# Talking-heads attention and two MLPs on one core: cosine's argument in turns, and all weights of the second MLP made float32 beside the first

## The chip, the core and the metric

The kernel runs on one core of a Trainium2 chip. The core has a matrix engine (TensorE: PE for its matmuls, PEld for the weight loads that run beside them), a vector engine (DVE), a scalar engine (ACT), GpSimd (POOL) and a queue of transfers that SyncE (SP) issues. Each engine takes its instructions strictly in the order in which they stand in its queue. An instruction that waits therefore holds everything behind it on that engine. The metric is the device time of one execution in microseconds (us), as the median of several runs.

## What is computed

All inputs are float32 or float64 arrays; the weights of both MLPs arrive as float64 and are used as float32. With 4 sequences of 448 tokens, 12 heads of 64:

```python
# attention with mixed heads
scores = q @ k.T / 8;  scores = einsum('bhij,hg->bgij', scores, w_pre)
attn = softmax(scores);  attn = einsum('bhij,hg->bgij', attn, w_post)
x = attn @ v                        # 1792 tokens x 768
# first MLP: 768 -> 2048 -> 768
h = x @ w_in;  g = h * cos(h);  y = g @ w_out
# second MLP: 768 -> 768 -> 768
h = maximum(maximum(y @ w1, y @ w2), y @ w3);  return h @ w_out
```

The names `moe_w_in`, `moe_w_out` belong to the first MLP, `moe2_w1` to `moe2_w3` and `moe2_w_out` (in the kernel `w_out2`) to the second.

## The kernel before

Activations are kept transposed: features on the 128 partitions, 448 tokens of one sequence in the free dimension. Every product is made from three matmuls with operands cut in a high and a low part (`three`, L191 to L195): high by high, low by high, high by low. So every tensor that enters a product is first cut: ACT casts the high part, and DVE or POOL subtracts it to get the low part.

Three stages follow each other. Attention has an order worked out by a planner from costs and due times (`Plan`, and the `add` calls in `attention`); it takes the span to about 500 us and is hardly touched here. The planner also places the first MLP's start, and its table of the steps of the cosine is the last part of the diff.

The first MLP (`layers`) runs over 8 groups of two hidden blocks, and in each over the 4 sequences: 32 steps. One step makes two hidden blocks of 128 features (36 matmuls), sends each through `times_cos`, and multiplies the result of the step before with w_out (36 matmuls), whose six results DVE adds to `acc`. A hidden block stays in PSUM until the cosine's product (`times`, L233) has read it. PSUM has 8 banks and a step takes 8 of them in turn, so the first hidden block of a step takes the bank that the first hidden block of the step before has left.

`times_cos` makes h*cos(h) in nine instructions. ACT writes h/2pi plus a large constant, which rounds it to whole turns (L216), and takes the constant off again (L219). DVE subtracts that many turns from h in two instructions, once with a short constant C1 and once with the rest C2 (both L224). ACT takes the size (L227) and the sine of pi/2 minus it (L230). DVE multiplies by h (L233), ACT casts the high part (L236), DVE makes the low one (L239).

Weights come as float64. One half row block (128 x 384 numbers) is loaded raw (384 KB), and an ACT and four DVE instructions make it float32. This happens at two places: in `weight_steps` (L130 to L146), just ahead of the weight's use, and in `float32_block` (L316 to L322), which makes a block and stores it in DRAM (L323) to be loaded later as float32 (192 KB, L312). Both use the same two buffers for raw data. In this text such a half block with its four DVE instructions is one conversion.

The second MLP takes two sequences at a time (p = 0, 1). It uses Strassen's scheme with 7 products for each of w1 to w3: `tokens` makes the token side (sums of quarters, each cut in high and low), `unit_weights` the weight side (L335 sums, L340 and L341 cuts), `unit` the 7 products p1 to p7. `unit` is run for 3 pairs of output blocks (j) and 3 weights (wi), so 9 times per p; the largest of the three is cut and multiplied with w_out2 in `out_product`, which is run for two sequences per j. `tokens` has 33 subtractions per p: 12 sums and 21 low parts, of which every third is on POOL (L365).

Of the 36 blocks of w1 to w3, `rest` converts 22 beside the first MLP (BEFORE, L472) and 14 in the first half of the second, two per unit (L486). The 12 half blocks of w_out2 are converted where they are used (L521), once for each p: 24 conversions. `tokens(0)` stands behind the first MLP's loop, `tokens(1)` behind the units of p = 0 (L480); the products with w_out2 of the last j of p = 0 come in the course of p = 1.

The order of the MLPs' instructions on each engine is made by a scheduler from the program's order and costs of its own, so a row of the code doesn't tell the place in a queue. The places that matter are shown as rows of the queues with the change.

Of the kernel before, what the change touches and what calls it, by code (L numbers as in the profile page):

```python
# [9 lines left out]
F32 = mybir.dt.float32  # L10
# [8 lines left out]
DM = H * D  # L19
# [14 lines left out]
KH = KC // 2  # L34
BEFORE = 22
FC = DFF // 128
NB = NT // S
TWO_PI = 2.0 * math.pi
C1 = 6.28125
C2 = TWO_PI - C1  # L40
ROUND = 1.5 * 2.0 ** 23
# [3 lines left out]
def f32(ap):  # L45
    return ap.bitcast(F32)


@with_exitstack
def talking_heads_mlps(ctx, tc, q, k, v, w_pre, w_post, same_row, w_in, w_out, w1, w2, w3, w_out2, outT):  # L50
    nc = tc.nc
    dram = ctx.enter_context(tc.tile_pool(name="dram", bufs=1, space=bass.MemoryType.DRAM))
    xT = dram.tile([DM, NT], F32, name="xT")

    tp = ctx.enter_context(tc.tile_pool(name="t", bufs=2, side="right", reuse_waits="tile"))
    mlps = Mlps(ctx, tc, xT, tp, w_in, w_out, (w1, w2, w3), w_out2, outT)
    mlps.kept = {(i, f): dram.tile([128, DM], F32, name=f"w{i}_{f}") for i in range(3) for f in range(KC)}
    with tc.manual_schedule(), ExitStack() as att:
        behind = attention(att, tc, q, k, v, w_pre, w_post, same_row, xT, tp, mlps)
    for ins in behind:  # L60
        ctx.enter_context(tc.issue_after(ins))
    mlps.rest()
# [7 lines left out]
class Mlps:  # L70
# [138 lines left out]
    def times_cos(self, pos, g, f):  # L209
# [10 lines left out]

        def less(c):
            if c == C1:
                o["r"] = self.tile("r", [128, S], F32)
            nc.vector.scalar_tensor_tensor(o["r"], o["k"], -c, h if c == C1 else o["r"], op0=ALU.mult, op1=ALU.add)  # L224

# [3 lines left out]
        def cos():  # L229
            nc.scalar.activation(o["r"], o["r"], AF.Sin, bias=self.half_pi, scale=-1.0)  # L230

# [8 lines left out]

        return [turns, whole, lambda: less(C1), lambda: less(C2), size, cos, times, high, low]

# [58 lines left out]
    def float32_block(self, src, keep=False):  # L301
# [3 lines left out]
        n = KH * 128  # L305
        w, kept = (x[:, c * n:(c + 1) * n] for x in (self.w123[wi][f], self.kept[wi, f]))
        float64 = w.dtype != F32
# [42 lines left out]
    def tokens(self, p):  # L350
# [3 lines left out]
        if p == 0:  # L354
            xs = [h for _ in range(3) for h in self.two_parts()]
            self.B = {x: halves(t) for x, t in zip(("11", "T1", "T2", "21", "T3", "T4"), xs)}
            self.outs = (lambda t: [t[:, :KC], t[:, KC:]])(self.tile("x", [128, 2 * KC, S], F32))
        y = {(r + 1, n + 1): self.acc[2 * p + n][:, r * KH:(r + 1) * KH] for r in range(2) for n in range(2)}
        turn = [0]

        def parts(x, c, src):
            hi, lo = (t[:, c] for t in self.B[x])
            nc.scalar.copy(hi, src)
            turn[0] += 1
            (nc.vector if turn[0] % 3 else nc.gpsimd).tensor_sub(lo, src, f32(hi))  # L365

# [93 lines left out]
    def rest(self):  # L460
        self.late = self.pools("late", "left")
        self.acc = [None] * NB
        self.spare = None
        blocks = [(wi, 2 * j + f, c) for j in range(KC // 2) for wi in range(3) for f in range(2) for c in range(2)]
        before = A = None
        first = self.layers(self.x, [(self.w_in[f],) for f in range(FC)], self.w_out, self.times_cos, self.to_y, self.GROUPS)
        steps = FC // self.GROUPS * NB
        for i, product in enumerate(first):
            if before:
                before()  # L470
            before = product
            while i > 1 and 36 - len(blocks) < BEFORE * (i - 1) / (steps - 4):  # L472
                self.float32_block(blocks.pop(0), True)
            if i == steps - 3:
                A = self.unit_weights(0, 0)
        ends, outs = [], [before]
        for p in range(NB // 2):
            run(ends)
            ends = []
            self.tokens(p)  # L480
            for j in range(KC // 2):
                most = {x: self.tile("kr"[i % 2], [128, S], F32) for i, x in enumerate(("11", "12", "21", "22"))}
                for wi in range(3):
                    p1, p5, p6, p2, p7, p4, p3 = self.unit(A or self.unit_weights(j, wi), wi, most)
                    A = None
                    for src in blocks[:2]:  # L486
                        self.float32_block(blocks.pop(0), True)
                    run([p1, p5])
# [29 lines left out]
                def outs_of(n, p=p, j=j, g=g, wo=wo, accs=self.outs):  # L518
                    if not wo:
                        self.spare = None  # L520
                        wo += [self.weight(self.w_out2[f]) for f in (2 * j, 2 * j + 1)]  # L521
                    self.out_product(2 * p + n, j, g[n], wo, accs[n])
# [76 lines left out]
def attention(ctx, tc, q, k, v, w_pre, w_post, same_row, xT, tp, mlps):  # L599
# [293 lines left out]
    for n in range(2):  # L893
# [3 lines left out]
        for c in range(KC):  # L897
            add(xhi, (n, c), r + 2.0 + c * RANK["fxgap"], {"A": 0.467}, [("xget", n)])
            add(xlo, (n, c), r + 2.0 + c * RANK["fxgap"], {"P": 1.09, "V": 0.535}, [("xhi", n, c)])
    acts = ({"A": 0.424}, {"A": 0.467}, {"V": 0.535}, {"V": 0.535}, {"A": 0.467}, {"A": 0.56}, {"V": 0.535}, {"A": 0.467}, {"V": 0.535})  # L900
    for f in range(FG):
        for c in range(KC):
            add(hidden, (f, c), r0 + RANK["fh"] + (f * KC + c) * RANK["fhgap"], {"T": 0.567},
                [("wcut", f, c // (KC // 2), 6), ("xlo", 0, c)] + ([("hidden", f, c - 1)] if c else [])
                + ([("act", f - 1, 6)] if f and c == 0 and BUFS["ps_x"] == 1 else []))
        for y, e in enumerate(acts):
            add(act, (f, y), r0 + RANK["fa"] + f + y * 0.2, e, [("act", f, y - 1) if y else ("hidden", f, KC - 1)]
                + [("soft", i) for i in range(N)] * (y == 5) + [("act", f - 1, 0)] * (f and y == 0))

# [47 lines left out]
```

## Time and profile before

| | us |
|---|---|
| median of 3 runs (lowest, highest) | 1353.25 (1352.34, 1357.11) |
| the profiled execution | 1349.79 |
| its span, first to last instruction | 1348.0 |
| PE busy / PEld busy | 1278.1 (95%) / 1056.2 (78%) |
| DVE / ACT / POOL busy | 1111.8 (82%) / 765.0 (57%) / 322.9 (24%) |

Matmuls are pipelined, so that a matmul shown with 0.37 us starts about 0.2 us after the one before it. Busy time of PE is therefore not its distance from full use; the count of matmuls in a stretch is. A wait in a row is the idle time of the engine before the instruction, and the arrow names the instruction whose end released it. The granted clock is a share of full speed: 1.00 is 2.4 GHz, 0.50 is 1.2 GHz.

### The profile page before, as it was taken

The numbers are of one execution on the slowest core, as the hardware profiler recorded it, in microseconds if no ns is written. First come the engines' busy times: TensorE is split into PE (matmuls) and PEld (weight loads), VectorE is DVE, ScalarE is ACT, GpSimd is POOL, SyncE is SP. The second block draws the span as 40 slices with busy tenths as digits, with TensorE's granted clock in tenths as the row PEclk, the third lists the DMA queues.
The fourth block names the chain that finished last, engine by engine and source line by source line (L and its number), as shares of the span: only waits on it lengthen the run. The fifth ranks groups of instructions, "written<-read, shape, count | busy, mean of one in ns | idle before, by whom it ended". The sixth has DMA issues, their size and how long they took to land. (4 is left out here: it accounts for less than half of the span.)

```text
span 1348.0 us, 20632 instructions
## 1 busy us (share of the span) xinstructions
PE 1278.1 (95%) x7002; PEld 1056.2 (78%) x7002; DVE 1111.8 (82%) x2276; ACT 765.0 (57%) x1697; POOL 322.9 (24%) x273
## 2 busy tenths in 40 slices
PE   7999999999999889999999999999979999899998
PEld 2676666676677668889888889999968888688988
DVE  1888787887878897899999989977889959988585
ACT  3877776776777777754554545535544444524440
POOL 0000010000100135221111111212255645645450
PEclk8999999999999999999999999999989999899999
DMA  6753444344343444533333333213024422134122
GB/s 206 198 160 95 123 137 141 112 121 127 108 123 101 127 122 151 141 88 112 104 90 95 94 88 88 71 48 95 8 84 144 118 71 60 47 118 129 47 77 82
DMA packets 81310, 143.09 MB, mean 106 GB/s; under 512 B 8789, under 2 KB 62645, under 8 KB 81205
## 3 DMA queue, kind: packets, MB, share of 16 engines
q1 hardware_dynamic: 81205, 141.78, 35.5%
q8 instruction: 55, 0.90, 0.3%
q14 instruction: 50, 0.41, 0.1%
HBM read 84.95 MB, written 18.09 MB: 76 GB/s over the span
## 5 line engine op out<-in xcount | busy, mean ns | idle before, releaser
L193 PE MATMUL ps<-x,w 128*128 128x448 f32 x708 | 266.3, 377 | 35.9 <-DVE r L233 12.0
L195 PE MATMUL ps<-x,w 128*128 128x448 f32 x708 | 262.4, 372 | 2.7 <-DVE x L176 0.8
L194 PE MATMUL ps<-x,w 128*128 128x448 f32 x708 | 262.4, 371 | 0.6 <-POOL w L152 0.6
L733 PEld LDWEIGHTS aps<-w2s,e 120*112 120x112 f32 x1440 | 164.1, 177 | 52.6 <-issue 20.2
L193 PE MATMUL ps<-gh,w 128*128 128x448 f32 x528 | 193.8, 367 | 1.5 <-DVE x L456 1.5
L194 PE MATMUL ps<-gh,w 128*128 128x448 f32 x528 | 193.4, 366 | 0.0
L195 PE MATMUL ps<-gl,w 128*128 128x448 f32 x528 | 193.2, 366 | 0.1
L733 PE MATMUL aps<-w2s,e 120*112 120x120 f32 x1440 | 179.8, 271 | 9.9 <-DVE w2s L728 6.9
L152 POOL TENSOR_TENSOR w<-wf,w 128x384 fp32r<-128x384 f32 x88 | 101.7, 1169 | 364.9 <-ACT w L149 309.0
L341 POOL TENSOR_TENSOR w<-wf,w 128x384 fp32r<-128x384 f32 x126 | 149.3, 1204 | 147.8 <-ACT w L340 112.8
L193 PEld LDWEIGHTS ps<-x,w 128*128 128x128 f32 x708 | 135.2, 191 | 59.4 <-DVE r L233 16.8
L195 PEld LDWEIGHTS ps<-x,w 128*128 128x128 f32 x708 | 135.3, 191 | 17.4 <-DVE x L365 2.3
L194 PEld LDWEIGHTS ps<-x,w 128*128 128x128 f32 x708 | 135.7, 192 | 11.8 <-POOL w L152 0.9
L711 DVE TENSOR_REDUCE nm<-mps 120x1 f32<-120x448 f32 x180 | 111.5, 620 | 36.6 <-PE mps L707 33.0
L716 ACT ACTIVATE e<-mps,nm 120x448 f32<-120x448 f32 x180 | 114.4, 636 | 41.1 <-DVE nm L711 32.4
L700 POOL TENSOR_TENSOR tl<-t,th 120x448 fp32r<-120x448 f32 x22 | 26.4, 1200 | 437.9 <-ACT th L615 292.7
L193 PEld LDWEIGHTS ps<-gh,w 128*128 128x128 f32 x528 | 99.2, 188 | 10.4 <-DVE x L456 1.9
L195 PEld LDWEIGHTS ps<-gl,w 128*128 128x128 f32 x528 | 99.2, 188 | 9.0 <-DVE gl L239 0.4
L194 PEld LDWEIGHTS ps<-gh,w 128*128 128x128 f32 x528 | 99.2, 188 | 8.1
L615 ACT CAST th<-t 120x448 fp32r<-120x448 f32 x167 | 94.3, 567 | 19.6 <-DMA t<-s 6.0
L340 ACT CAST w<-wf 128x384 fp32r<-128x384 f32 x126 | 61.0, 513 | 77.3 <-DVE wf L335 27.2
L700 DVE TENSOR_TENSOR tl<-t,th 120x448 fp32r<-120x448 f32 x158 | 100.3, 635 | 2.3 <-ACT th L615 2.0
(107 smaller groups left out, 2348.7 us busy)
## 6 DMA issues: line engine op xcount, KB each, us to landing
t<-s SPq DMA_DIRECT2D x144, 192.5 KB
wraw<-in_w_out_dram SPq DMA_DIRECT2D x56, 384.0 KB
wraw<-in_w_dram SPq DMA_DIRECT2D x36, 384.0 KB
wf<-w SPq DMA_DIRECT2D x72, 192.0 KB
wraw<-in_w_in_dram SPq DMA_DIRECT2D x32, 384.0 KB
t<-s SPq DMA_DIRECT2D x48, 210.0 KB
w<-wf SPq DMA_DIRECT2D x36, 192.0 KB
q<-in_q_dram SPq DMA_DIRECT2D x48, 112.0 KB
```

The costliest lines, as they stand in the source:

```text
L152: nc.gpsimd.tensor_sub(lo, chunks(o["f"]), f32(hi))
L193: mm(w[0], x[0], start=first, stop=False)
L194: mm(w[1], x[0], start=False, stop=False)
L195: mm(w[0], x[1], start=False, stop=last)
L340: nc.scalar.copy(hi, w)
L341: nc.gpsimd.tensor_sub(lo, w, f32(hi))
L615: copy = lambda eng, *a: nc.scalar.copy(*a) if eng == "A" else any_of[eng].tensor_copy(*a)
L700: any_of[eng].tensor_sub(live["tl", i], live["t", n][:P, t, :], f32(live["th", i]))
L711: nc.vector.tensor_reduce(nm, live["m", i][:P], axis=AX.X, op=ALU.max, negate=True)
L716: nc.scalar.activation(e, live["m", i][:P], AF.Exp, bias=live["nm", i], scale=1.0, accum_out=z)
L733: nc.tensor.matmul(ps[:JC, j], live["e", i][:, j * JC:(j + 1) * JC], live["w2s", i], start=True, stop=True)
```

## The change

The cosine's argument is taken in turns: one DVE instruction makes h/2pi minus the whole turns, and the sine gets the factor 2pi as its scale. `times_cos` has eight steps instead of nine. All 48 blocks of the second MLP's weights, those of w_out2 among them, are made float32 beside the first MLP, from step 4 on, 48 of them over 28 steps; the second MLP only loads float32. `unit_weights(0, 0)` moves one step ahead, `tokens(0)` moves from behind the loop to the step before the last, all 21 low parts of `tokens` are on DVE, and at p = 1 the remaining products with w_out2 come ahead of `tokens(1)`.

```diff
@@ times_cos
-        def less(c):
-            if c == C1:
-                o["r"] = self.tile("r", [128, S], F32)
-            nc.vector.scalar_tensor_tensor(o["r"], o["k"], -c, h if c == C1 else o["r"], op0=ALU.mult, op1=ALU.add)
+        def part_of_turn():
+            o["r"] = self.tile("r", [128, S], F32)
+            nc.vector.scalar_tensor_tensor(o["r"], h, 1.0 / TWO_PI, o["k"], op0=ALU.mult, op1=ALU.subtract)
...
-            nc.scalar.activation(o["r"], o["r"], AF.Sin, bias=self.half_pi, scale=-1.0)
+            nc.scalar.activation(o["r"], o["r"], AF.Sin, bias=self.half_pi, scale=-TWO_PI)
...
-        return [turns, whole, lambda: less(C1), lambda: less(C2), size, cos, times, high, low]
+        return [turns, whole, part_of_turn, size, cos, times, high, low]
@@ float32_block
-        w, kept = (x[:, c * n:(c + 1) * n] for x in (self.w123[wi][f], self.kept[wi, f]))
+        w, kept = (x[:, c * n:(c + 1) * n] for x in ((*self.w123, self.w_out2)[wi][f], self.kept[wi, f]))
@@ tokens
-            turn[0] += 1
-            (nc.vector if turn[0] % 3 else nc.gpsimd).tensor_sub(lo, src, f32(hi))
+            nc.vector.tensor_sub(lo, src, f32(hi))
@@ rest
-        blocks = [(wi, 2 * j + f, c) for j in range(KC // 2) for wi in range(3) for f in range(2) for c in range(2)]
+        blocks = [(wi, 2 * j + f, c) for j in range(KC // 2) for wi in range(4) for f in range(2) for c in range(2)]
...
-            while i > 1 and 36 - len(blocks) < BEFORE * (i - 1) / (steps - 4):
+            while i > 3 and 48 - len(blocks) < 48 * (i - 3) / (steps - 4):
                 self.float32_block(blocks.pop(0), True)
-            if i == steps - 3:
+            if i == steps - 4:
                 A = self.unit_weights(0, 0)
+            if i == steps - 2:
+                self.tokens(0)
...
-            self.tokens(p)
+            if p:
+                run(outs)
+                outs = []
+                self.tokens(p)
...
-                    for src in blocks[:2]:
-                        self.float32_block(blocks.pop(0), True)
...
-                        wo += [self.weight(self.w_out2[f]) for f in (2 * j, 2 * j + 1)]
+                        wo += [self.weight(self.kept[3, f] if self.w_out2.dtype != F32 else self.w_out2[f]) for f in (2 * j, 2 * j + 1)]
@@ attention: the planner's table of the cosine's steps loses one DVE step
-    acts = ({"A": 0.424}, {"A": 0.467}, {"V": 0.535}, {"V": 0.535}, {"A": 0.467}, {"A": 0.56}, {"V": 0.535}, {"A": 0.467}, {"V": 0.535})
+    acts = ({"A": 0.424}, {"A": 0.467}, {"V": 0.535}, {"A": 0.467}, {"A": 0.56}, {"V": 0.535}, {"A": 0.467}, {"V": 0.535})
```

DVE's queue before, at the end of the first MLP. The cosine steps (L224, L233, L239) of the last hidden blocks stand ahead of most of `tokens(0)`, whose sums are L371 and L373 and whose low parts are L365; L283 are the first MLP's last additions to `acc`:

```order
L224 SCALAR_TENSOR_TENSOR r<-k,ps 128x448
L233 TENSOR_TENSOR r<-ps,r 128x448
L224 SCALAR_TENSOR_TENSOR r<-k,r 128x448
L283 TENSOR_TENSOR acc<-ps,acc 128x448
L239 TENSOR_TENSOR gl<-r,gh 128x448
L283 TENSOR_TENSOR acc<-ps,acc 128x448
L233 TENSOR_TENSOR r<-ps,r 128x448
L283 TENSOR_TENSOR acc<-ps,acc 128x448 x2
L239 TENSOR_TENSOR gl<-r,gh 128x448
L283 TENSOR_TENSOR acc<-ps,acc 128x448
L365 TENSOR_TENSOR x<-k,x 128x448
L373 TENSOR_TENSOR r<-acc,k 128x448
```

DVE's queue now at the same place (L375 and L358 are the sums and low parts of `tokens(0)`, L220, L229 and L235 the cosine, L279 the additions):

```order
L358 TENSOR_TENSOR x<-r,x 128x448 x2
L358 TENSOR_TENSOR x<-k,x 128x448
L375 TENSOR_TENSOR r<-acc 128x448 x2
L358 TENSOR_TENSOR acc<-acc 128x448
L358 TENSOR_TENSOR x<-r,x 128x448 x2
L358 TENSOR_TENSOR acc<-acc 128x448 x2
L220 SCALAR_TENSOR_TENSOR r<-ps,k 128x448 x2
L279 TENSOR_TENSOR acc<-ps,acc 128x448 x2
L229 TENSOR_TENSOR r<-ps,r 128x448
L279 TENSOR_TENSOR acc<-ps,acc 128x448
L229 TENSOR_TENSOR r<-ps,r 128x448
L235 TENSOR_TENSOR gl<-r,gh 128x448
```

The cosine of the last two hidden blocks and the last additions now stand behind the whole of `tokens(0)`.

DVE's queue before, in the last third of the second MLP (j = 2 of p = 1). L410 and L412 take the units' results out of PSUM, L335 are sums of weights, and L134 to L146 convert w_out2:

```order
L410 TENSOR_TENSOR r<-ps,acc 128x448
L146 SCALAR_TENSOR_TENSOR wf<-wf,wt 128x384
L335 TENSOR_TENSOR wf<-wf 128x384
L146 SCALAR_TENSOR_TENSOR wf<-wf,wt 128x384
L134 TENSOR_SCALAR wt<-wraw 128x384
L138 SCALAR_TENSOR_TENSOR wt<-wraw,wt 128x384
L142 SCALAR_TENSOR_TENSOR wt<-wraw,wt 128x384
L146 SCALAR_TENSOR_TENSOR wf<-wf,wt 128x384
L134 TENSOR_SCALAR wt<-wraw 128x384
L410 TENSOR_TENSOR r<-ps,acc 128x448
```

And now, from the same place on (L403 and L405 take out results, L430 takes a maximum, L331 are sums of weights):

```order
L403 TENSOR_TENSOR k<-ps,acc 128x448
L331 TENSOR_TENSOR wf<-wf 128x384
L403 TENSOR_TENSOR r<-ps,acc 128x448
L331 TENSOR_TENSOR wf<-wf 128x384
L403 TENSOR_TENSOR r<-ps,acc 128x448
L403 TENSOR_TENSOR acc<-ps,acc 128x448
L405 TENSOR_TENSOR k<-acc,k 128x448
L403 TENSOR_TENSOR acc<-ps,acc 128x448
L405 TENSOR_TENSOR r<-acc,r 128x448
L430 TENSOR_TENSOR k<-ps,k 128x448
```

No conversion stands in the second MLP any more; between two results only sums of weights are left.

## Rows read from the trace of the kernel before

**Rows 1.** Busy time of each engine by stage; columns as in the head row.

```profile
core 0: us, PE busy (x) PEld busy (x) DVE busy (x) ACT busy (x) POOL busy (x), PEclk, DMA share, GB/s
540.00:800.00 260.00, 247.14 (x1199) 224.00 (x1198) 243.86 (x450) 141.69 (x281) 46.74 (x41) 1.00 0.35 102
800.00:950.00 150.00, 150.00 (x737) 138.19 (x736) 127.92 (x234) 75.42 (x144) 24.15 (x21) 1.00 0.25 73
955.00:1010.00 55.00, 48.21 (x219) 42.60 (x218) 47.74 (x77) 27.84 (x56) 22.24 (x17) 0.94 0.18 52
1010.00:1150.00 140.00, 132.70 (x632) 118.74 (x631) 116.86 (x166) 62.96 (x134) 77.75 (x65) 0.99 0.33 97
1150.00:1180.00 30.00, 23.55 (x100) 19.39 (x99) 26.95 (x37) 16.83 (x35) 20.60 (x17) 0.89 0.19 52
1180.00:1345.00 165.00, 157.49 (x759) 142.81 (x757) 118.91 (x176) 56.38 (x117) 67.72 (x59) 0.99 0.29 89
```

**Rows 2.** PE's first hidden matmuls, 540 to 800 us: busy, mean ns, idle before.

```profile
L193 PE MATMUL ps<-x,w 128*128 128x448 f32 x195 | 72.9, 374 | 12.9 <-DVE r L233 12.0 <-DVE acc L266 0.8
```

**Rows 3.** Timeline: PE's waits in the second MLP; start, us, instruction, idle before.

```profile
996.37 0.74 PE L193 MATMUL ps<-x,w 128*128 128x448 f32 x1 [5.96 <-DVE acc L283]
...
1034.90 0.47 PE L193 MATMUL ps<-x,w 128*128 128x448 f32 x1 [2.63 <-ACT acc L431]
...
1158.20 0.74 PE L193 MATMUL ps<-x,w 128*128 128x448 f32 x1 [4.62 <-ACT x L363]
...
1292.64 0.74 PE L193 MATMUL ps<-x,w 128*128 128x448 f32 x1 [3.22 <-DVE r L410]
```

**Rows 4.** Timeline: conversions in front of two of these waits, ACT and DVE.

```profile
1033.87 0.56 ACT L316 ACTIVATE wf<-wraw 128x384 f32<-128x384 f32 x1 [1.16 <-POOL w L341]
...
1289.89 1.23 DVE L142 SCALAR_TENSOR_TENSOR wt<-wraw,wt 128x384 int32<-128x384 int32 x1
...
1291.97 0.62 DVE L410 TENSOR_TENSOR r<-ps,acc 128x448 f32<-128x448 f32 x1
```

**Rows 5.** DVE's groups, 540 to 800 us: the cosine's second subtraction and conversions.

```profile
L224 DVE SCALAR_TENSOR_TENSOR r<-k,r 128x448 f32<-128x448 f32 x34 | 27.8, 817 | 0.2
...
L134 DVE TENSOR_SCALAR wt<-wraw 128x384 int32<-128x384 int32 x41 | 18.6, 458 | 7.9 <-DMA wraw<-in_w_in_dram 5.8 <-DMA wraw<-in_w_out_dram 2.0
L320 DVE SCALAR_TENSOR_TENSOR wt<-wraw,wt 128x384 int32<-128x384 int32 x16 | 10.1, 644 | 0.2
L321 DVE SCALAR_TENSOR_TENSOR wt<-wraw,wt 128x384 int32<-128x384 int32 x16 | 9.4, 598 | 0.3
L322 DVE SCALAR_TENSOR_TENSOR wf<-wf,wt 128x384 f32<-128x384 f32 x16 | 8.7, 551 | 0.2
L318 DVE TENSOR_SCALAR wt<-wraw 128x384 int32<-128x384 int32 x16 | 7.6, 485 | 2.7 <-DMA wraw<-in_w_dram 2.7
```

**Rows 6.** Timeline around the first token pass: PE, then DVE, then POOL.

```profile
960.82 0.37 PE L193 MATMUL ps<-x,w 128*128 128x448 f32 x1
...
975.38 0.37 PE L193 MATMUL ps<-x,w 128*128 128x448 f32 x1
...
963.47 1.15 DVE L283 TENSOR_TENSOR acc<-ps,acc 128x448 f32<-128x448 f32 x2
...
978.67 0.62 DVE L376 TENSOR_TENSOR k<-acc,r 128x448 f32<-128x448 f32 x1
979.20 0.61 DVE L365 TENSOR_TENSOR x<-r,x 128x448 fp32r<-128x448 f32 x1
...
987.63 1.98 DVE L382 TENSOR_TENSOR r<-acc 128x448 f32<-128x448 f32 x2
...
989.09 1.53 POOL L365 TENSOR_TENSOR x<-k,x 128x448 fp32r<-128x448 f32 x1
```

**Rows 7.** Timeline: one cosine on DVE, from its second subtraction to its product.

```profile
969.20 0.62 DVE L224 SCALAR_TENSOR_TENSOR r<-k,r 128x448 f32<-128x448 f32 x1
...
971.49 0.62 DVE L233 TENSOR_TENSOR r<-ps,r 128x448 f32<-128x448 f32 x1
```

More of the change, by code (lines that the diff above doesn't have):

```diff
@@ L34 @@
 KH = KC // 2
-BEFORE = 22
 FC = DFF // 128
@@ L38 @@
 TWO_PI = 2.0 * math.pi
-C1 = 6.28125
-C2 = TWO_PI - C1
 ROUND = 1.5 * 2.0 ** 23
@@ L56, in talking_heads_mlps @@
     mlps = Mlps(ctx, tc, xT, tp, w_in, w_out, (w1, w2, w3), w_out2, outT)
-    mlps.kept = {(i, f): dram.tile([128, DM], F32, name=f"w{i}_{f}") for i in range(3) for f in range(KC)}
+    mlps.kept = {(i, f): dram.tile([128, DM], F32, name=f"w{i}_{f}") for i in range(4) for f in range(KC)}
     with tc.manual_schedule(), ExitStack() as att:
@@ L356, in tokens @@
             self.B = {x: halves(t) for x, t in zip(("11", "T1", "T2", "21", "T3", "T4"), xs)}
-            self.outs = (lambda t: [t[:, :KC], t[:, KC:]])(self.tile("x", [128, 2 * KC, S], F32))
         y = {(r + 1, n + 1): self.acc[2 * p + n][:, r * KH:(r + 1) * KH] for r in range(2) for n in range(2)}
-        turn = [0]
         def parts(x, c, src):
@@ L471, in rest @@
             before = product
-            while i > 1 and 36 - len(blocks) < BEFORE * (i - 1) / (steps - 4):
+            while i > 3 and 48 - len(blocks) < 48 * (i - 3) / (steps - 4):
                 self.float32_block(blocks.pop(0), True)
-            if i == steps - 3:
+            if i == steps - 4:
                 A = self.unit_weights(0, 0)
+            if i == steps - 2:
+                self.tokens(0)
+        out = self.tile("x", [128, 2 * KC, S], F32)
+        self.outs = [out[:, :KC], out[:, KC:]]
         ends, outs = [], [before]
@@ L904, in attention @@
                 [("wcut", f, c // (KC // 2), 6), ("xlo", 0, c)] + ([("hidden", f, c - 1)] if c else [])
-                + ([("act", f - 1, 6)] if f and c == 0 and BUFS["ps_x"] == 1 else []))
+                + ([("act", f - 1, 5)] if f and c == 0 and BUFS["ps_x"] == 1 else []))
         for y, e in enumerate(acts):
             add(act, (f, y), r0 + RANK["fa"] + f + y * 0.2, e, [("act", f, y - 1) if y else ("hidden", f, KC - 1)]
-                + [("soft", i) for i in range(N)] * (y == 5) + [("act", f - 1, 0)] * (f and y == 0))
+                + [("soft", i) for i in range(N)] * (y == 4) + [("act", f - 1, 0)] * (f and y == 0))
     plan.run({**BUFS, "t": 2, "tl": BUFS["th"], "ps": BUFS["ps_s"] + BUFS["ps_x"]})
```

## The prediction

> **What bounds the kernel now.** I read the busy times by stage first [rows 1]. From 800 to 950 us PE is never idle and starts 737 matmuls in 150 us, one every 0.2035 us; that is its pace at the full clock, and the counts of the other stretches are measured with it. From 540 to 800 us, also first MLP, 1199 matmuls would take 244.0 of 260 us: 16.0 us are lost. In the second MLP the four stretches would take 44.6 of 55, 128.6 of 140, 20.4 of 30 and 154.5 of 165 us: 10.4, 11.4, 9.6 and 10.5 us are lost, 41.9 together. So PE bounds both MLPs, and the whole room for a change that takes no matmul away is these 58 us.
>
> Next, the waits of PE say who holds it. In the first MLP it is nearly always L233, the cosine's product, which gives the PSUM bank back: 12.0 of 12.9 us of idle time [rows 2], in pieces of about one us. DVE is busy 243.86 of 260 us there [rows 1], so its queue runs late. In the second MLP the waits are few and long [rows 3]: 5.96 us behind the first token pass, 4.62 behind the second, 2.63 and 3.22 at units in between. The last two have conversions ahead of them [rows 4]: ACT's copy L431 stood behind L316 of a conversion that came late, and L410 ran at 1291.97 us right behind the shifts of w_out2. The granted clock is 0.94 and 0.89 in the stretches of the two passes [rows 1]: after these idle times the level of 1.2 GHz is granted for some microseconds, and the first matmul shows 0.74 us where after a shorter wait it shows 0.47 [rows 3]. This loss is part of the sums above.
>
> **The change, part by part.**
>
> *The cosine and the blocks in the first MLP.* Each step loses two L224 of 0.817 us, 1.63 us [rows 5]. A conversion costs 0.485 + 0.644 + 0.598 + 0.551 = 2.28 us of DVE [rows 5]. Between 540 and 800 us there are 57 of them (41 and 16) in 260 / (72 x 0.2035) = 17.7 steps: 3.2 per step. In the changed kernel's order the steps 9 to 27 carry an even 3.8 per step. That adds 0.6 x 2.28 = 1.4 us to the 13.8 us of DVE per step, less 1.63: about as full as before, 13.6 of the 14.65 us that PE takes. The chain of a cosine is also one instruction shorter: L224 to the end of L233 takes 2.9 us [rows 7], with the second subtraction 0.62 of them. I let the loss of 16.0 us fall to 13. From 800 to 950 us it is other: before, 2.25 conversions per step stood there by the order, now 3.5, so DVE rises from 12.5 to 12.5 + 1.25 x 2.28 - 1.63 = 13.7 us per step, the load at which the earlier stretch lost 16.0 / 17.7 = 0.9 us per step. Over ten steps that is 9 us at most and none at least; I take 5. Together the first MLP gets 2 us slower; bounds 9 slower (13 stays 16, and 9) and 16 faster (all waits gone). The added loads of raw data make DVE wait on average (7.9 + 2.7) / 57 = 0.19 us per conversion [rows 5]; that is in the 0.9 us.
>
> *The first token pass.* Its 33 DVE instructions now stand ahead of the cosine of the last two hidden blocks, and PE needs their banks for p1 of the first unit. PE has the last hidden blocks (from 960.82 us) and one product with w_out to do until 975.38 us [rows 6]. After the last addition of the product before, which in this trace ends at 964.6 us [rows 6], 25 instructions of the pass are left in the new order. At the pace of 0.53 us, at which they start where nothing disturbs them [rows 6], they end at 977.9, at 0.62 us each at 980.1. Then a cosine takes 2.9 us less the subtraction that is gone, but two subtractions stand in a row, so 2.9 us again [rows 7]: the bank comes free at 980.8 to 983.0, and PE waits 5.4 to 7.6 us. Before, it waited 5.96 at a later place and lost 10.4 in all. If the additions come a few us earlier, as an emptier DVE allows, the wait is 3. I take 5, with 1.5 for the lower clock: 6.5 instead of 10.4, a gain of 4. Behind this wait stand, on DVE, the additions that free the other six banks, and on PE all units. Bounds: 9 gained, and 5 lost, if half of the 25 go at the 0.99 us that each of two sums took beside POOL at 987.63 [rows 6]: 25 x 0.76 = 19 us, the bank free at 986.5, a wait of 11.1, and on top the 4.4 that came on top of the wait before (10.4 - 5.96).
>
> *A rule on the moved low parts.* Two sums took 1.98 us while POOL worked, three times the pace, and POOL's own low part took 1.53 [rows 6]. Seven of 21 low parts per pass go from POOL to DVE. The Trainium skill, Perfetto Trace Analysis, section "Optimizing Scalar/DVE Operations", says that GpSimd and DVE share an SBUF read port, so that moving work between the two might not help. By that rule the seven gain nothing and the pass goes on at its disturbed pace, which is the bound of 5 lost, 9 us worse than my sum. The row agrees on the sharing; but it is POOL's work beside DVE that makes DVE slow, and with the low parts gone from POOL I expect little of it there. The case stands below as a rival.
>
> *Conversions out of the second MLP.* 14 blocks and 24 of w_out2, 38 x 4 DVE and 38 ACT instructions, leave. From 1010 to 1150 us the loss of 11.4 falls to 4.5, from 1180 on from 10.5 to 5. What then is late next are the weights' cuts: seven POOL subtractions per unit, 65 in 140 us at 77.75 us busy [rows 1], 55% of POOL, enough cover; and the loads, which now are 192 KB where w_out2 had 384. The 12 transfers of the output (half of p = 0) now stand in one piece in SP's queue, ahead of loads for the second and third unit of p = 1, and go out at PE's pace. These loads are needed some 18 us after the last of them, so this is hidden. Gain 6.9 + 5.5 = 12.4; bounds 5 and 19.
>
> *The second token pass.* Two more products (72 matmuls, 14.7 us) now stand between the last unit and p1, and in the new order the pass alternates with their additions; behind the last addition 11 of its instructions are left, and p1, p5, p6 and p2 run beside them. 9.6 falls to 2: gain 7.6; bounds 3 and 9.6.
>
> *Sum.* 4 + 12.4 + 7.6 - 2 = 22 us off the profiled execution's 1349.8 (span 1348.0 and 1.8 around it), 1327.8. The median lies 3.45 us above that execution, so 1331.
>
> **Rivals.**
>
> *DVE becomes the bound of the first MLP: slower.* The place is every step from 4 to 28. It decides from where DVE's work and its waits for raw data pass 14.65 us per step. At the 1.23 us that a shift takes beside POOL [rows 4] a conversion would cost 0.49 + 3 x 1.23 = 4.2 us, 0.6 of them 2.5, and the step 13.8 - 1.63 + 2.5 + 0.9 = 15.6: 24 steps x 0.95 = 23 us more, and the first pass 5 worse, against 20 gained: 1361. For it: DVE at 94% already. Against it: POOL is busy only 18% in that stretch [rows 1], and the means already hold that.
>
> *The first token pass blocks PE.* As bounded above, 5 lost instead of 4 gained: 1340. For it, the order itself. Against it, POOL has little to do there.
>
> *The second MLP finds another limit.* POOL's cuts or the loads take over half of what the conversions leave: half of 12.4 and of 7.6 is lost: 1341. For it, one wait names ACT and not DVE.
>
> *The first MLP's waits go too.* The shorter chain frees the banks in time: 16 less instead of 2 more: 1316 with a little of it left.
>
> **How the numbers follow.** A measurement of this kernel can tell about 0.5% (6.8 us) from no change. Forecast 0.52 (own range 1323 to 1337), second MLP limited 0.17, first pass blocks 0.13, better than forecast 0.10, slower 0.08. The first four are faster by over 6.8 us, but 0.05 of the limited second MLP ends above 1346.5 and 0.01 of the slower case below 1360: faster 0.87, same 0.06, slower 0.07. The range of 1316 to 1346 leaves out the slower case, the far end of the limited second MLP, and a little below.
>
> **What would show it.** Right: the matmuls of the second MLP's stretches lose under 20 us against 0.2035 us each, no raw load behind the first MLP, no long wait of PE at the second pass, and one of 3 to 8 us on L229, the cosine's product, at the first p1. In the first MLP PE's waits on that product go on past 800 us, but stay about one us. Wrong: waits of over 1 us in every step, DVE over 97% busy from 540 to 950 us, or units of the second MLP that wait for cuts on POOL or for loads.

## The result and the profile after

The changed kernel takes 1332.01 us (median of 4 runs, 1330.71 to 1332.9), the kernel before 1353.3 (1352.34 to 1357.11) beside it. The ratio is 0.9837, with a 95% interval of 0.9815 to 0.9858: faster, by 1.4 to 1.9%. The profiled execution took 1330.71 us with a span of 1329.0, so 19 us less than the span before.

First the busy times of the engines by stage, the answer to [rows 1]. The stages of the second MLP begin and end at other times now.

```profile
core 0: us, PE busy (x) PEld busy (x) DVE busy (x) ACT busy (x) POOL busy (x), PEclk, DMA share, GB/s
540.00:800.00 260.00, 247.73 (x1193) 223.57 (x1192) 238.69 (x453) 143.48 (x282) 40.64 (x36) 0.99 0.45 127
800.00:950.00 150.00, 143.01 (x690) 130.04 (x689) 127.52 (x243) 78.20 (x150) 23.87 (x22) 0.99 0.37 101
985.00:1020.00 35.00, 31.29 (x146) 28.42 (x145) 21.05 (x35) 15.21 (x31) 14.44 (x14) 0.95 0.16 45
1020.00:1160.00 140.00, 138.55 (x675) 125.85 (x674) 89.56 (x127) 60.04 (x125) 72.23 (x64) 1.00 0.22 67
1160.00:1190.00 30.00, 27.19 (x125) 24.23 (x124) 21.97 (x35) 13.80 (x29) 16.15 (x15) 0.94 0.31 100
1190.00:1326.00 136.00, 135.42 (x664) 124.10 (x662) 74.20 (x104) 46.47 (x97) 55.30 (x51) 1.00 0.21 66
```

At 0.2035 us a matmul, the losses are 17.2 and 9.6 us in the two stretches of the first MLP (before 16.0 and 0), and 5.3, 2.6, 4.6 and 0.9 us in the second (before 10.4, 11.4, 9.6 and 10.5). So the second MLP gained and the first gave back. Three points of PE's timeline say the same without counting. They are the first matmul of the first MLP, the last matmul of the product of step 30 (the steps count from 0), and the last matmul of all; here before, then after (the middle one of after is the first line of the timeline of the second MLP further down):

```profile
470.35 0.46 PE L193 MATMUL ps<-x,w 128*128 128x448 f32 x1
...
975.18 0.37 PE L195 MATMUL ps<-gl,w 128*128 128x448 f32 x1
...
1344.13 0.36 PE L195 MATMUL ps<-gl,w 128*128 128x448 f32 x1
```

```profile
472.07 0.45 PE L190 MATMUL ps<-x,w 128*128 128x448 f32 x1
...
1325.06 0.36 PE L192 MATMUL ps<-gl,w 128*128 128x448 f32 x1
```

The product of step 30 ends at 975.5 us before and at 985.5 after, 10.0 later. From there to the last matmul it takes 369.0 us before (to 1344.5) and 339.9 after (to 1325.4), 29.1 less. 29.1 - 10.0 is the whole difference. Of the 10.0, 1.7 lie ahead of the first MLP, which starts at 470.3 us before and at 472.1 after. These 1.7 us are not shown to come from the change: on DVE, ACT and POOL the same instructions stand in the same order up to there, and the other kernels of this document in which that holds start the first MLP at 470.4 to 473.2 us.

PE's first hidden matmuls after, from 540 to 800 us, the answer to [rows 2] (busy, mean ns, idle before):

```profile
L190 PE MATMUL ps<-x,w 128*128 128x448 f32 x194 | 73.1, 377 | 12.3 <-DVE r L229 12.2
```

Nearly all of the wait is again for the cosine's product (now L229). From 540 to 950 us together it is 19.1 us; before it was the 12.9 us of [rows 2], since PE lost nothing from 800 to 950 us.

The timeline of PE in the second MLP, the answer to [rows 3]:

```profile
985.16 0.37 PE L192 MATMUL ps<-gl,w 128*128 128x448 f32 x1
989.24 0.47 PE L190 MATMUL ps<-x,w 128*128 128x448 f32 x1 [3.71 <-DVE acc L279]
...
1038.33 0.47 PE L190 MATMUL ps<-x,w 128*128 128x448 f32 x1 [1.39 <-ACT acc L424]
...
1165.40 0.47 PE L192 MATMUL ps<-x,w 128*128 128x448 f32 x1 [1.18 <-DVE x L358]
1167.50 0.74 PE L190 MATMUL ps<-x,w 128*128 128x448 f32 x1 [1.63 <-ACT acc L409]
```

These four are all its waits of over one us there. 5.96 became 3.71, 4.62 became 1.18 and 1.63, and of the waits at units, behind conversions before [rows 4], only the 1.39 us is left.

The first token pass on DVE, from its 25 last instructions' first to what comes behind them, the answer to [rows 6]:

```profile
972.33 0.62 DVE L366 TENSOR_TENSOR r<-acc,k 128x448 f32<-128x448 f32 x1
...
975.67 1.44 DVE L366 TENSOR_TENSOR r<-acc,k 128x448 f32<-128x448 f32 x1
...
986.43 1.16 DVE L358 TENSOR_TENSOR acc<-acc 128x448 fp32r<-128x448 f32 x2
987.50 1.16 DVE L220 SCALAR_TENSOR_TENSOR r<-ps,k 128x448 f32<-128x448 f32 x2
988.56 1.15 DVE L279 TENSOR_TENSOR acc<-ps,acc 128x448 f32<-128x448 f32 x2
989.62 0.62 DVE L229 TENSOR_TENSOR r<-ps,r 128x448 f32<-128x448 f32 x1
```

The pass ends at 987.59 us, 25 instructions in 15.2 us, and p1 starts right behind the first addition after it (988.56), not behind the product L229.

DVE's groups from 540 to 800 us, the answer to [rows 5]: the one subtraction of the cosine, and the first step of a conversion (L131 for the first MLP's own weights, L314 for blocks).

```profile
L220 DVE SCALAR_TENSOR_TENSOR r<-ps,k 128x448 f32<-128x448 f32 x33 | 20.4, 618 | 0.2 <-ACT k L216 0.2
...
L131 DVE TENSOR_SCALAR wt<-wraw 128x384 int32<-128x384 int32 x34 | 15.3, 450 | 8.0 <-DMA wraw<-in_w_in_dram 4.6 <-DMA wraw<-in_w_out_dram 3.3
L314 DVE TENSOR_SCALAR wt<-wraw 128x384 int32<-128x384 int32 x34 | 13.1, 385 | 3.6 <-DMA wraw<-in_w_dram 2.6 <-DMA wraw<-in_w_out_dram 0.6
```

The 817 ns subtraction is gone, there are 68 conversions for 57, and DVE's own standing at raw loads is 11.6 us for 10.6. By this row alone the loads look free.

Last, where the first MLP's time went. ScalarE's first step of a conversion, the size of the high words, from 540 to 950 us; of the kernel before (L130 for the first MLP's own weights, L316 for blocks), then of the one after (L127, L312):

```profile
L130 ACT ACTIVATE wf<-wraw 128x384 f32<-128x384 f32 x53 | 29.4, 554 | 40.8 <-DMA wraw<-in_w_in_dram 22.0 <-DMA wraw<-in_w_out_dram 17.7 <-POOL w L152 0.9
L316 ACT ACTIVATE wf<-wraw 128x384 f32<-128x384 f32 x24 | 13.3, 553 | 22.1 <-DMA wraw<-in_w_dram 15.6 <-POOL w L341 3.3 <-POOL w L152 2.5
```

```profile
L127 ACT ACTIVATE wf<-wraw 128x384 f32<-128x384 f32 x51 | 28.4, 557 | 32.5 <-DMA wraw<-in_w_in_dram 18.5 <-DMA wraw<-in_w_out_dram 13.6
L312 ACT ACTIVATE wf<-wraw 128x384 f32<-128x384 f32 x47 | 26.1, 555 | 65.7 <-DMA wraw<-in_w_dram 45.7 <-DMA wraw<-in_w_out_dram 15.2 <-POOL w L337 3.0
```

77 became 98 conversions, and ScalarE's standing before them rose from 63 to 98 us. One load followed through the queues after shows what that does; timelines of SP, ACT, DVE and PE:

```profile
855.85 0.33 SPq L311 DMA_DIRECT2D wraw<-in_w_dram  x1
```

```profile
859.07 0.56 ACT L312 ACTIVATE wf<-wraw 128x384 f32<-128x384 f32 x1 [5.21 <-DMA wraw<-in_w_dram]
859.53 0.53 ACT L213 ACTIVATE k<-ps 128x448 f32<-128x448 f32 x1
...
863.21 0.67 ACT L226 ACTIVATE r<-r,half_pi 128x448 f32<-128x448 f32 x1
```

```profile
860.64 1.38 DVE L318 SCALAR_TENSOR_TENSOR wf<-wf,wt 128x384 f32<-128x384 f32 x1
861.95 0.61 DVE L220 SCALAR_TENSOR_TENSOR r<-ps,k 128x448 f32<-128x448 f32 x1
862.48 0.65 DVE L314 TENSOR_SCALAR wt<-wraw 128x384 int32<-128x384 int32 x1
...
864.88 0.62 DVE L229 TENSOR_TENSOR r<-ps,r 128x448 f32<-128x448 f32 x1
```

```profile
865.55 0.47 PE L190 MATMUL ps<-x,w 128*128 128x448 f32 x1 [2.38 <-DVE r L229]
```

The load is issued when one of the two raw buffers comes free: its last reader, L317 of the block before, ends at 855.79 us. ScalarE can go on behind the load 3.2 us after its issue began (855.85 to 859.07). PE had finished the hidden tile at about 855.9; its first cosine step L213 runs at 859.53, behind L312, which waited for the load. On DVE the subtraction then stands behind a block's last step, and the product behind all four of the next block. PE waits 2.38 us. This is one load; whether the loads set the time of the whole stage is for the experiments.

### The profile page after: what moved, and what is told of

Its sections match the earlier page's. It is cut to its first block, busy times and chain, and to the rows that moved or that the text cites. A ratio compares the mean times of both kernels' runs of the same rounds, so it can differ in the third digit from the quotient of the medians.

```text
span 1329.0 us, 20579 instructions
## 1 busy us (share of the span) xinstructions
PE 1273.8 (96%) x7002; PEld 1055.8 (79%) x7002; DVE 1029.5 (77%) x2180; ACT 763.5 (57%) x1684; POOL 289.0 (22%) x258
## 5 line engine op out<-in xcount | busy, mean ns | idle before, releaser
L190 PE MATMUL ps<-x,w 128*128 128x448 f32 x708 | 265.3, 375 | 26.0 <-DVE r L229 19.1
L337 POOL TENSOR_TENSOR w<-wf,w 128x384 fp32r<-128x384 f32 x126 | 139.8, 1133 | 191.0 <-ACT w L336 131.2
L149 POOL TENSOR_TENSOR w<-wf,w 128x384 fp32r<-128x384 f32 x88 | 99.2, 1138 | 367.5 <-ACT w L146 225.5
L192 PEld LDWEIGHTS ps<-x,w 128*128 128x128 f32 x708 | 134.6, 190 | 15.2 <-DVE x L358 1.6
L331 DVE TENSOR_TENSOR wf<-wf 128x384 f32<-128x384 f32 x72 | 61.0, 856 | 63.6 <-DMA wf<-w 49.7
```

What stands on the lines that cost most here:

```text
L149: nc.gpsimd.tensor_sub(lo, chunks(o["f"]), f32(hi))
L190: mm(w[0], x[0], start=first, stop=False)
L192: mm(w[0], x[1], start=False, stop=last)
L331: f(raw[x], raw[l], raw[r])
L337: nc.gpsimd.tensor_sub(lo, w, f32(hi))
```

## The experiments

Two theories of the first MLP. A: VectorE has more work with 48 blocks, and its amount sets the pace. B: the two raw buffers and the 3.2 us of a load make ScalarE and VectorE stand at raw loads, in order, with cosines behind them. All medians are to be compared with 1332.0 for the change; the kernel before, run beside each, gave 1352.4 to 1352.7. "First MLP" is from its first matmul to the end of the product of step 30, "rest" from there to the last matmul, of the profiled execution (before 505.2 and 369.0 us, after 513.5 and 339.9).

**The new cosine alone.** In the kernel before, with the sine's factor and the planner's table as in the change:

```
-            nc.vector.scalar_tensor_tensor(o["r"], o["k"], -c, h if c == C1 else o["r"], op0=ALU.mult, op1=ALU.add)
+            nc.vector.scalar_tensor_tensor(o["r"], h, 1.0 / TWO_PI, o["k"], op0=ALU.mult, op1=ALU.subtract)
```

> The kernel before with the new cosine alone (22 blocks beside the first MLP, the token pass behind it as before). Theory A, VectorE's amount of work sets the first MLP's pace: 64 instructions of 0.76 us go, TensorE's idle at the first products (12.9 us from 540 to 800) falls under 5 us and the first MLP ends 6 to 12 us earlier, so 1341 to 1347 us. Theory B, the waits come from ScalarE and VectorE standing in order at a block's raw load, in front of the next cosine: these stay, only each chain is 0.76 us shorter, and the first MLP ends 0 to 5 us earlier, 1348 to 1353 us. Both: nothing changes in the second MLP.

1344.56 us, ratio 0.9943 (0.9923 to 0.9963). First MLP 495.6, rest 372.9; that the rest is 3.9 us longer than before was in neither expectation, and its cause was not sought. PE's first hidden matmuls from 540 to 950 us:

```profile
L191 PE MATMUL ps<-x,w 128*128 128x448 f32 x324 | 120.2, 371 | 5.2 <-DVE r L230 5.2
```

The wait was 12.9 us before from 540 to 800 us alone [rows 2]. By A's numbers: one instruction less in each cosine is worth 9.6 us of the first MLP where 22 blocks stand beside it. ScalarE stood 67 us ahead of its conversion steps in this run (63 in the kernel before), and PE waited little all the same.

**The old cosine in the changed kernel.** Again with its factor and the planner's table:

```
-            nc.vector.scalar_tensor_tensor(o["r"], h, 1.0 / TWO_PI, o["k"], op0=ALU.mult, op1=ALU.subtract)
+            nc.vector.scalar_tensor_tensor(o["r"], o["k"], -c, h if c == C1 else o["r"], op0=ALU.mult, op1=ALU.add)
```

> The changed kernel with the old cosine of two subtractions (48 blocks beside the first MLP). VectorE gets 64 instructions of about 0.76 us back, 43 us from 540 to 950, where it was busy 366 of 410 us. Theory A: VectorE is then full and the first MLP ends 10 to 25 us later, 1342 to 1357 us. Theory B: part of it falls into the time in which VectorE stands at loads, 2 to 8 us later, 1334 to 1340 us.

1346.92 us, 0.9964 (0.995 to 0.9978): in A's range, but not by A's way. The first MLP is 517.6, 4.1 longer, as B had it. So the same instruction is worth 9.6 us beside 22 blocks and 4.1 beside 48. The rest is 351.9, 12.0 longer, of it 9.7 at p1 of the first unit; six blocks were still to be converted after 950 us, where the changed kernel has one:

```profile
1003.05 0.74 PE L192 MATMUL ps<-x,w 128*128 128x448 f32 x1 [13.41 <-DVE acc L282]
```

**Blocks without their loads.** 48 raw loads are left out, and the blocks convert what the first MLP's own weights have left in their buffer, so that the second MLP computes with other weights:

```
-                    o["raw"] = self.tile("wraw", [128, n * 128, 2], I32)
+                    o["raw"] = self.raw = self.tile("wraw", [128, n * 128, 2], I32)
...
-        raw = self.tile("wraw", [128, n, 2], I32)
-        nc.sync.dma_start(raw, w.bitcast(I32).rearrange("p (n t) -> p n t", t=2))
+        raw = self.raw
```

> The changed kernel, but a block's conversion reads the raw weights that the last conversion of the first MLP's own weights left in their buffer, so that the 48 loads of raw blocks are left out (the blocks hold other weights); every instruction of VectorE and ScalarE stays. Theory A, the amount of work: the first MLP stays within 3 us of the changed kernel's, 1329 to 1335 us. Theory B, the loads: ScalarE's idle time at the block's size step (66.5 us from 540 to 975) falls under 15 us, TensorE's idle at the first products from 19 to under 9 us from 540 to 950, and the time to 1318 to 1325 us.

1314.56 us, 0.9727 (0.9699 to 0.9754), still less than B had. First MLP 497.7, rest 339.4. PE's and ACT's rows from 540 to 950 us:

```profile
L190 PE MATMUL ps<-x,w 128*128 128x448 f32 x324 | 119.7, 369 | 9.0 <-DVE r L229 9.0
```

```profile
L311 ACT ACTIVATE wf<-wraw 128x384 f32<-128x384 f32 x48 | 25.4, 553 | 17.8 <-DMA w<-wf 6.6 <-DVE wt L139 5.0 <-POOL w L149 3.2
```

All 240 instructions of the blocks on DVE and ACT are still there, and the first MLP is 15.8 us shorter, even shorter than before the change. For the blocks A does not explain the loss: 15.8 us go with their loads, with every instruction in place. What the instructions would cost by themselves was not tried. The edit takes away three things at once, the waits for the loads, the blocks' use of the two buffers and the traffic; the run with three buffers below bears on the last.

**One instruction less in each conversion.** The last three bits of the fraction are left out:

```
-        nc.vector.scalar_tensor_tensor(t, raw[:, :, 0], 29, t, op0=ALU.logical_shift_right, op1=ALU.bitwise_or)
```

> The changed kernel with one of the four VectorE instructions of each block's conversion left out (the last three bits of the fraction): 48 instructions of 0.6 us, 29 us of VectorE's time in the first MLP. Theory A: the first MLP ends 7 to 14 us earlier, 1318 to 1325 us. Theory B: the loads are waited for as before, and it ends 0 to 4 us earlier, 1328 to 1332 us.

1332.93 us, 0.9857 (0.9836 to 0.9878): no gain. First MLP 515.2, rest 340.7. PE waits 19.3 us for the product as before. DVE's first step of a block, 540 to 950 us, in the changed kernel, then in this one:

```profile
L314 DVE TENSOR_SCALAR wt<-wraw 128x384 int32<-128x384 int32 x47 | 18.0, 383 | 5.1 <-DMA wraw<-in_w_dram 3.8 <-DMA wraw<-in_w_out_dram 0.8
```

```profile
L314 DVE TENSOR_SCALAR wt<-wraw 128x384 int32<-128x384 int32 x47 | 20.5, 439 | 17.7 <-DMA wraw<-in_w_dram 15.3 <-DMA wraw<-in_w_out_dram 2.2
```

VectorE was busy 22.3 us less from 540 to 950 us (343.9 for 366.2) and stood that much longer, 12.6 us of it at this load. That is B's mark.

**The size step on GpSimd.** 48 times, squared against the squared bound:

```
-        nc.scalar.activation(o, f32(raw[:, :, 1]), AF.Abs)
+        nc.gpsimd.tensor_tensor(o, f32(raw[:, :, 1]), f32(raw[:, :, 1]), op=ALU.mult)
```

> The changed kernel, but the 48 blocks' first step, the size of the high word (0.56 us each on ScalarE, which stood 65.7 us at it from 540 to 950), is a square on GpSimd, compared with the squared bound; loads and VectorE's work stay. Theory B1, the load is waited for at the head of ScalarE's queue with the next cosine's k behind it: the first MLP ends 6 to 12 us earlier, 1319 to 1326 us. Theory B2, the wait moves to VectorE's first step of the block, which reads the same load and has the cosine's product behind it: 1328 to 1334 us. If the two engines disturb each other, VectorE's instructions grow by a tenth or more and it takes over 1336 us.

1345.05 us, 0.9945 (0.9925 to 0.9965), the third of the cases. First MLP 526.3. DVE's second step of a block was 561 ns in the changed kernel, from 540 to 950 us, and is:

```profile
L316 DVE SCALAR_TENSOR_TENSOR wt<-wraw,wt 128x384 int32<-128x384 int32 x45 | 32.8, 729 | 1.0
```

The four steps of a block together went from 2.18 to 2.47 us, 13% more. So this run could not tell ScalarE's wait from VectorE's: it added a cost of its own.

**The size step left out.** A block ends after DVE's third step, without the flush of numbers too small for float32:

```
-        nc.scalar.activation(o, f32(raw[:, :, 1]), AF.Abs)
-        t = self.tile("wt", [128, n], I32)
+        t = o.bitcast(I32)
...
-        nc.vector.scalar_tensor_tensor(o, o, F64_TINY, f32(t), op0=ALU.is_ge, op1=ALU.mult)
```

> The changed kernel; a block's conversion leaves out the flush of numbers too small for float32: ScalarE's size step and VectorE's last step, 48 of each (0.56 and 0.63 us), and ends after VectorE's third. All loads, stores and buffers stay, but ScalarE no longer reads a block. Theory B1, ScalarE stands at the loads in front of the next cosine: TensorE's idle at the first products falls from 19 to under 9 us from 540 to 950, 1318 to 1324 us. Theory C, the load is waited for by whichever engine reads it first and VectorE has the cosine behind it just as ScalarE had: 1328 to 1333 us, as in the run with one instruction of VectorE less.

1322.99 us, 0.9786 (0.9769 to 0.9802): B1's time, but not its mark; PE's wait fell to 14.1 us and not under 9. First MLP 505.8. DVE now stands at the block's load itself:

```profile
L313 DVE TENSOR_SCALAR wf<-wraw 128x384 int32<-128x384 int32 x48 | 20.8, 433 | 24.2 <-DMA wraw<-in_w_dram 18.4 <-DMA wraw<-in_w_out_dram 4.5 <-POOL w L335 1.3
```

Half of what the loads cost is gone (7.7 of 15.8 us), and VectorE's standing at a block's first step has grown from 5.1 to 24.2 us, which is the likely place of the other half. Theory C's time was missed as well.

**Three raw buffers.** The float32 number is made in the output's buffer and its size in the raw one, which frees room for a third:

```
-    PLACES = {"x": (2, 4), "w": (3, 7), "wraw": (2, 2), "wf": (2, 6), "wt": (1, 2),
+    PLACES = {"x": (2, 4), "w": (3, 7), "wraw": (2, 3), "wf": (2, 6),
...
+        t, hi = o.bitcast(I32), f32(raw[:, :, 1])
...
+        nc.scalar.activation(hi, hi, AF.Abs)
+        nc.vector.scalar_tensor_tensor(o, hi, F64_TINY, o, op0=ALU.is_ge, op1=ALU.mult)
```

The same is done with the first MLP's own weights, and the planner's table follows the new order of the steps.

> The changed kernel with three raw buffers in the place of two; the room comes from making the float32 number in the output's own buffer and its size in the raw one, so that the size step comes behind VectorE's first three. A load is then issued one conversion earlier. Theory B or C, the wait for loads 2.9 us after their issue out of two buffers: ScalarE's and VectorE's idle time at raw loads falls by half or more, and the first MLP ends 5 to 12 us earlier, 1320 to 1327 us. Rival: the conversion's longer chain through ScalarE holds each buffer as much longer as the third one gives, 1329 to 1338 us.

(The 2.9 us count from the end of the issue, the 3.2 above from its start.) 1320.55 us, 0.976 (0.9745 to 0.9775): faster than the changed kernel, the intervals are apart. First MLP 505.6, 7.9 shorter, rest 342.0; another 4.2 us lie ahead of the first MLP, which starts at 467.9 us; the order there is the planner's new one, but kernels of one order differ by 2.8 us at this point, so only a part may be the edit's. Rows from 540 to 950 us, PE, then DVE's first steps, then ACT's size step of a block:

```profile
L191 PE MATMUL ps<-x,w 128*128 128x448 f32 x322 | 119.6, 372 | 12.7 <-DVE r L230 12.6
```

```profile
L314 DVE TENSOR_SCALAR wf<-wraw 128x384 int32<-128x384 int32 x48 | 24.0, 510 | 10.4 <-DMA wraw<-in_w_dram 5.0 <-POOL w L338 2.4 <-DMA w<-wf 2.3
L131 DVE TENSOR_SCALAR wf<-wraw 128x384 int32<-128x384 int32 x51 | 19.5, 391 | 1.7 <-DMA wraw<-in_w_in_dram 1.0 <-DMA wraw<-in_w_out_dram 0.5
```

```profile
L318 ACT ACTIVATE wraw<-wraw 128x384 f32<-128x384 f32 x47 | 25.9, 559 | 49.4 <-DVE wf L316 49.3
```

No engine stands long at a raw load now (6.5 us on DVE). ScalarE still stands 49.4 us at this step, for DVE's steps ahead of it, and the gain came all the same. So its idle time as such is not the price; what counts is, as far as these runs go, what a late load puts in front of a cosine. The traffic of the loads is not the price either, at least of these 7.9 us: all loads are still there. But the edit does two things, it adds a buffer and moves the size step behind VectorE's first three, and neither was tried by itself. From 540 to 800 us DVE is now busy 250.9 of 260 us, so its amount of work is the likeliest cause of what PE still waits; that was not tried.

**Fewer blocks beside the first MLP.**

```
+        later = [b for b in blocks if b[0] == 3 and b[1] > 1]
+        blocks = [b for b in blocks if b not in later]
+        n = len(blocks)
...
-            while i > 3 and 48 - len(blocks) < 48 * (i - 3) / (steps - 4):
+            while i > 3 and n - len(blocks) < n * (i - 3) / (steps - 4):
...
+                    for _ in range(2 if wi == 0 else 1):
+                        if p == 0 and later:
+                            self.float32_block(later.pop(0), True)
```

> The changed kernel with 28 blocks beside the first MLP instead of 48; the other 20 of the last weights, w_out2, are converted in the first half of the second MLP, two, one and one in the three units of a pass. Theory B, the loads: one block in a step instead of two, the first MLP ends 8 to 13 us earlier; the second MLP, where VectorE is busy 90 of 140 us, takes 20 x 2.4 us of VectorE's work and gets back 1 to 6 us; 1321 to 1330 us. Theory A, that conversions cost wherever they stand: the second MLP is 10 us or more longer, 1331 to 1338 us.

1340.27 us, 0.9912 (0.9895 to 0.9928). The edit does not do what I expected of it. w_out2 has 12 blocks, and `later` takes 8 of them, so that 40 stay beside the first MLP and not 28. Eight blocks fewer did not shorten it (514.3), so the cost of a block is not an even share of the whole; what 28 would do was not tried. The rest became 345.6, 5.7 longer, with a wait of 3.96 us at 1043.10 us where the changed kernel has 1.39. For the second MLP, where the 8 blocks now stand, it is one more sign that conversions there cost.

**The first token pass behind the loop.**

```
-            if i == steps - 2:
-                self.tokens(0)
...
+        self.tokens(0)
         ends, outs = [], [before]
```

> The changed kernel with the first token pass written behind the first MLP's loop, where the kernel before had it, not one step ahead of its end. If the earlier place is what took the 5.96 us in front of p1 down to 3.71: the pass starts 5 to 8 us later, TensorE waits 6 to 12 us for it, and the time is 1334 to 1341 us. If the order is set by the work's own dependences and not by the place: 1329 to 1333 us.

1331.09 us, 0.9846 (0.9829 to 0.9863): no difference. PE's longest wait there is 3.11 us. The earlier place of the pass, part of the change, is worth nothing that can be measured.

**The two output products behind the second pass.**

```
             if p:
-                run(outs)
-                outs = []
                 self.tokens(p)
```

> The changed kernel with the two last output products of the first half left behind the second token pass, as in the kernel before, instead of ahead of it. My working of the change: their 7.5 us of TensorE's work each is what covers the pass; without it the waits there grow from 2.8 us back to 8 to 11 us (the kernel before lost 9.6 us there), 1335 to 1340 us. Rival: GpSimd's third of the low parts made the pass slow before, not the order; then 1330 to 1334 us.

1335.17 us, 0.9873 (0.9858 to 0.9888), the lower edge of my working. Rest 344.2, 4.3 longer. PE's wait at the pass is back, though at 3.7 us and 0.8 more behind it, not the 8 to 11 that I had expected:

```profile
1154.20 0.47 PE L190 MATMUL ps<-x,w 128*128 128x448 f32 x1 [3.70 <-ACT x L357]
```

**A third of the low parts on GpSimd again.**

```
-            nc.vector.tensor_sub(lo, src, f32(hi))
+            turn[0] += 1
+            (nc.vector if turn[0] % 3 else nc.gpsimd).tensor_sub(lo, src, f32(hi))
```

> The changed kernel with every third low part of the token passes on GpSimd again (6 of 18 in each). If GpSimd beside VectorE is what made the passes long before: the first pass, 15.2 us of VectorE's, takes 18 us or more though it has 6 instructions less, p1 waits 6 us or more in the place of 3.71, and the second pass loses 3 us more; 1336 to 1343 us. If only the number of instructions counts: VectorE has 3.7 us less in each pass, 1327 to 1332 us.

1329.61 us, 0.9831 (0.9817 to 0.9846): with the changed kernel within the intervals. The first pass, DVE and POOL:

```profile
970.51 0.61 DVE L368 TENSOR_TENSOR r<-acc,k 128x448 f32<-128x448 f32 x1
...
978.59 1.57 DVE L377 TENSOR_TENSOR r<-acc 128x448 f32<-128x448 f32 x1
...
985.34 0.61 DVE L279 TENSOR_TENSOR acc<-ps,acc 128x448 f32<-128x448 f32 x1
985.87 1.02 DVE L360 TENSOR_TENSOR acc<-acc 128x448 fp32r<-128x448 f32 x1
```

```profile
978.14 1.54 POOL L360 TENSOR_TENSOR x<-k,x 128x448 fp32r<-128x448 f32 x1
```

(It is 7 of 21 low parts in each pass, not the 6 of 18 that I wrote.) 21 instructions of the pass take 15.8 us on DVE, where 25 took 15.2: the four fewer bought nothing, since sums beside POOL's low parts and weight cuts take 1.3 to 1.6 us. p1 waits only 1.81 us, but because an addition now stands ahead of the pass's last instructions (985.34). Neither expectation had that way.

**Three raw buffers and the third on GpSimd.** Both edits together.

> Both gains together: three raw buffers (1320.55 us, its first token pass unchanged, p1 waiting 3.71 us) and every third low part of the token passes on GpSimd (1329.61 us, p1 waiting 1.81 us). If the two places are independent, as they lie 35 us and more apart: p1 waits under 2.2 us and the time is 1317 to 1319.5 us. If GpSimd's third gains only what the first MLP's late end gives it: 1320 to 1322 us.

1322.6 us, 0.9763 (0.9739 to 0.9787): no better than three raw buffers alone, and just above both expected ranges. p1 waits 3.81 us here, so the 1.81 was an accident of that order. The best version found is the one with three raw buffers.

## Why the prediction came out, point by point

The time (1331 against 1332.0) is right, but partly by luck, since errors cancelled: the first MLP ends 10.0 us later where I said 2, and the rest is 29.1 shorter where I said 24. For the profiled execution that makes 1330.7 where I had 1327.8; and the median lies only 1.3 us above it, where I had carried over 3.45.

*First MLP: the mis-sized term.* I let DVE's instructions decide, and put the added loads aside with "that is in the 0.9 us". The cosine alone gives 9.6 us, so the 26 more blocks cost 8.3 + 9.6 = 17.9 us beside it (beside the old cosine 517.6 - 505.2 = 12.4), and 15.8 come back when the loads of all 48 are left out; what the loads of the first 22 cost before was not tried. My 0.19 us of waiting per conversion was DVE's own idle time [rows 5]; most of the standing at loads was on ACT, a row that I did not read. That row alone would not have given the price either, since ACT stood 67 us there with the new cosine alone, where PE's wait was down to 5.2. The bound of 9 slower held for the MLP itself (8.3), with the 1.7 us of later start beside it. The rival that DVE becomes the bound named the right place and the wrong price: PE waited over one us in every second or third step, but DVE was no busier (366.2 us from 540 to 950, 371.8 before).

*First token pass.* Gain 5.1 by stage, forecast 4; the wait of 3.71 us is in the range. The releaser was the addition L279 and not the product L229. That the order made the gain is not borne out: with the pass behind the loop the time is the same. What else gave it wasn't tried by itself.

*Conversions out of the second MLP.* 8.8 + 9.6 us by stage, forecast 12.4 and at most 19: right in kind, too low. The losses of 4.5 and 5 us that I left in these stretches had no working behind them. Both stretches end at nearly the pace of PE, 2.6 and 0.9 us off; POOL's cuts and the loads held nobody, so that rival is out. The run with the cosine alone kept these losses (rest 372.9).

*Second token pass.* 9.6 fell to 4.6, not to 2. The products ahead of it cover 4.3 us (rest 344.2 without them), as the run shows; two waits stayed, one for a low part of the pass (L358) and one for the copy of p1's result (L409).

*The rule on the shared port.* "Three times the pace" was misread: two sums in 1.98 us are 0.99 each, against 0.53 to 0.62 under twice. The Trainium skill, Perfetto Trace Analysis, section "Optimizing Scalar/DVE Operations", says that moving work between GpSimd and DVE might not help. The runs agree both ways: a block's steps got 13% longer beside more work on GpSimd, and seven low parts moved there left the pass as long as it was. My rival took the rule to mean a slow pass in the changed kernel; with POOL nearly idle only two sums were slow (1.44 and 1.33 us, beside POOL's two weight cuts from 975.30 to 977.99), and the rival fell.

*Left open.* How the loads' cost divides between ScalarE's and VectorE's standing: the run without ScalarE's step took a step of VectorE away too, and with three buffers the steps stand in another order. And the second MLP's gain by a run: that the conversions are most of it is argued from what is left, since undoing the place of the first pass and the low parts cost nothing and undoing the place of the output products 4.3 us. No run put the 38 conversions back by themselves.

## What to carry over

Count a conversion by its load as well as by its instructions: with two buffers and a load of 3.2 us against 2.2 us of VectorE's work on it, taking an instruction out of each conversion only lengthened the wait, and a third buffer, with the size step moved, was worth 7.9 us of the first MLP. Before moving work beside a stage, look at the idle column of every engine that reads the new data first, not only of the engine that is fullest, and at what stands behind each of these waits. Undo the parts of a change one by one even when the sum fits, since here two errors of 5 to 8 us hid each other.

## What the hardware showed beside this

After PE's wait of 2.38 us at 865.55 the granted clock fell to its lower level, 1.2 GHz, for some 3.4 us. The first row is ahead of the fall, the second within it:

```profile
851.00:865.00 14.00, 12.17 (x61) 10.98 (x59) 13.34 (x25) 7.38 (x15) 2.31 (x2) 1.00 0.43 127
867.00:870.00 3.00, 3.00 (x10) 2.66 (x9) 2.30 (x6) 1.52 (x4) 0.00 (x0) 0.50 0.25 94
```

Matmuls start 0.37 us apart there and not 0.20. The ten starts from 866.88 us on take 3.59 us where they would take 2.04. The same followed the wait of 2.19 us at 706.23, and not the one of 1.78 at 816.34. The length of the wait alone does not decide it: without the size step the clock fell after a wait of 1.78 us at 705.07 and not after one of 2.90 at 580.90. So a late load can cost PE more than its wait, about 1.6 us on top, but need not.
